# Seven products by whole batches: the last phase of an attention and feed-forward kernel, rearranged

## The chip, the cores and the metric

The kernel runs on one core of a Trainium2 chip. A core has TensorE (matrix products, results in PSUM), VectorE, ScalarE, GpSimd and DMA queues; each works through its own list of instructions, and semaphores tie the lists together. In profile lines they are PE (with PEld for its weight loads), DVE, ACT, POOL and SP. The metric is the device time of one execution in microseconds (us), as the median of several runs.

## What is computed

Routed attention is followed by a feed-forward block. Cut to what matters here:

```python
# attention: batch 4, heads 8, seq 768, head_dim 64; attn_out (4, 8, 768, 64)
x = attn_out.transpose(0, 2, 1, 3).reshape(3072, 512)
h = x @ w_in                                  # (3072, 512) @ (512, 2048)
g = h * (1.0 / (1.0 + np.exp(-1.702 * h)))    # a quick gelu
return (g @ w_out).astype(np.float32)         # (3072, 2048) @ (2048, 512)
```

Attention of all four batches and the feed-forward block of batch 0 lie in the earlier phases. The last phase, which is changed, does the feed-forward block of batches 1, 2 and 3. All matrix products are in float32; the profile has two matmul records for each one in the program.

## The kernel before

In the last phase both products are done in the way of Strassen and Winograd: each matrix is cut into 2 x 2 blocks, and seven products of blocks and of sums of blocks take the place of eight. A11 to A22 are the blocks of the left side, S1 to S4 sums of them; B11 to B22 and T1 to T4 the same of the right side; C11 to C22 are the blocks of the result. In the first layer A is w_in (by halves of the 2048 hidden features and of the 512 inputs) and B is x transposed (by halves of the inputs and of a batch's tokens). In the second layer A is the hidden layer g and B is w_out. P is 128, HALF 384, NF 16, FB 8, DM 512, DN 256, NH 3, B 4. A *group* is a batch and one of three parts of 128 token columns from both halves; there are nine groups.

```python
def sum_up(engine, A, S, side=0):
    if side == 0:
        todo = ((S[1], A[21], A[22], ALU.add),
                (S[2], S[1], A[11], ALU.subtract),
                (S[4], A[12], S[2], ALU.subtract),
                (S[3], A[11], A[21], ALU.subtract))
    else:
        todo = ...                       # cut: the four sums of a right side
    for o, a, b, op in todo:
        engine.tensor_tensor(out=o, in0=a, in1=b, op=op)

def seven(product, C):                   # the order of both layers
    def add(o, p, a):
        nc.vector.tensor_tensor(out=o, in0=p, in1=a, op=ALU.add)
    p = product(lambda A, S: A[11], lambda B, T: B[11])
    nc.scalar.copy(C[11], p)
    p = product(lambda A, S: S[2], lambda B, T: T[2])
    add(C[22], p, C[11])
    p = product(lambda A, S: S[1], lambda B, T: T[1])
    add(C[12], p, C[22])
    p = product(lambda A, S: S[3], lambda B, T: T[3])
    add(C[21], p, C[22]); add(C[22], p, C[12])
    yield 22
    p = product(lambda A, S: S[4], lambda B, T: B[22])
    add(C[12], p, C[12])
    yield 12
    ...                                  # cut: A22 T4 to C21, A12 B21 to C11

def first7(i, quad):                     # four chunks of 128 features, 128 columns
    ...
    def product(a, x):
        ps = ps_b.tile([P, 512], FP32, name="b")
        for f in range(4):
            for c in range(2):
                nc.tensor.matmul(out=ps[:, f * P:(f + 1) * P], lhsT=a(*ws[4 * quad + f, c]),
                                 rhs=x(*xs[c]), start=(c == 0), stop=(c == 1))
        return ps
    ...
    for k in seven(product, C):
        t = th.tile([P, 4 * P], FP32, name="th")
        gelu(C[k], t, C[k])   # ScalarE: tanh(1.702 h); VectorE: (tanh + 1) * h

def second7(i):
    ...
    def product(a, z):
        ps = bank()
        for f in range(FB):
            nc.tensor.matmul(out=ps[:, 0:DN], lhsT=a(*gs[f // 4])[:, f % 4 * P:(f % 4 + 1) * P],
                             rhs=z(*zs[f])[:, 0], start=(f == 0), stop=(f == FB - 1))
        return ps[:, 0:DN]
    for k in seven(product, C):
        ...                              # cut: store this quarter of the result

for c in range(2):
    sum_up(nc.vector, *W(c, 0, 4 * P))   # sums of w_in, kept for the whole phase
sums_x(0)
for c in range(2):
    sum_up(nc.vector, *W(c, 4 * P, FB * P))
sums_x(1)
while ffn:
    ffn.popleft()()                      # what is left of batch 0
...                                      # cut: ok and ok1, the check of the row sums
for f in range(0, FB, 2):
    sum_up(nc.gpsimd, *Z(f, f + 2), 1)   # sums of w_out
first7(0, 0)
for i in range(len(groups)):
    last = i == len(groups) - 1
    sums_g(i, 0)                         # VectorE: sums of g
    first7(i, 1)
    sums_g(i, 1)
    first7(i + 1, 0)
    sums_x(i + 2)
    if last:
        ...                              # cut: transpose of ok1, okt, bad
        is_bad = nc.values_load(bad[0:1, 0:1], min_val=0, max_val=1)
    second7(i)
```

The value is_bad decides at the end whether a general version runs in addition; with these inputs it does not. ScalarE's tanh and VectorE's product after it are the gelu of h / 2, since attention leaves x halved.

Of the kernel before, what the change touches and what calls it, by code (L numbers as in the profile page):

```python
# [8 lines left out]
FP32 = mybir.dt.float32  # L9
# [5 lines left out]
ALU = mybir.AluOpType  # L15
AX = mybir.AxisListType
# [22 lines left out]
def fast(  # L39
# [26 lines left out]
    nc = tc.nc  # L66

    B, H, S, D = q.shape
    NC = centroids.shape[1]
    DM, DF = moe_w_in.shape  # L70
# [36 lines left out]
    def bank():  # L107
        return ps_m.tile([P, 512], FP32, name="m")
# [117 lines left out]

    hot = hp1.tile([P, NJ * 4, 32], BF16, name="hot")
    nc.vector.memset(hot, 0.0)
    sums = const.tile([P, 2, 2 * NPAIR], FP32, name="sums")

# [240 lines left out]
    def check(g):  # L473


        rec = recs.pop(g)
        nc.scalar.activation(out=rec, in_=rec, func=AF.Copy,
                             accum_out=sums[:, 0, g:g + 1])
        nc.scalar.activation(out=rec, in_=rec, func=AF.Relu, bias=top[:, 0:1],
                             scale=-2.0 * LIMIT * LIMIT,  # L480
                             accum_out=sums[:, 1, g:g + 1])


    def gelu(g, t, h):

        nc.scalar.activation(out=t, in_=h, func=AF.Tanh, scale=1.702)  # L486
        nc.vector.scalar_tensor_tensor(out=g, in0=t, scalar=1.0, in1=h,  # L487
                                       op0=ALU.add, op1=ALU.mult)
# [111 lines left out]
    for t in range(NT + 2):  # L600
# [39 lines left out]
        if second_half and t % 2:  # L640
# [15 lines left out]
    FB = NF // 2  # L656
    DN = DM // 2
    sp = ctx.enter_context(tc.tile_pool(name="sp", bufs=1))
    tp = ctx.enter_context(tc.tile_pool(name="tp", bufs=2))
    gb = ctx.enter_context(tc.tile_pool(name="gb", bufs=18))  # L660
    th = ctx.enter_context(tc.tile_pool(name="th", bufs=1))
    ps_b = ctx.enter_context(tc.tile_pool(name="ps_b", bufs=5, space=PS))
    W_of = {(i, c): sp.tile([P, FB * P], FP32, name=f"W{i}{c}")
            for i in (1, 2, 4) for c in range(2)}
    Z_of = {i: sp.tile([P, FB, DN], FP32, name=f"Z{i}") for i in (2, 3, 4)}
    groups = [(b, n) for b in range(1, B) for n in range(NH)]

    def sum_up(engine, A, S, side=0):

        if side == 0:  # L670
            todo = ((S[1], A[21], A[22], ALU.add),
                    (S[2], S[1], A[11], ALU.subtract),
                    (S[4], A[12], S[2], ALU.subtract),
                    (S[3], A[11], A[21], ALU.subtract))
        else:
            todo = ((S[3], A[22], A[12], ALU.subtract),
                    (S[1], A[12], A[11], ALU.subtract),
                    (S[2], A[22], S[1], ALU.subtract),
                    (S[4], A[21], S[2], ALU.subtract))
        for o, a, b, op in todo:  # L680
            engine.tensor_tensor(out=o, in0=a, in1=b, op=op)  # L681

    def W(c, lo, hi):

        A = {10 * (r + 1) + m + 1: w_in[:, 2 * m + c, r * FB * P + lo:
                                        r * FB * P + hi]
             for r in range(2) for m in range(2)}
        S = {i: W_of[i, c][:, lo:hi] for i in (1, 2, 4)}
        S[3] = A[21]
        return A, S  # L690

    def Z(lo, hi):

        Bs = {10 * (r + 1) + m + 1: w_out[:, r * FB + lo:r * FB + hi,
                                          m * DN:(m + 1) * DN]
              for r in range(2) for m in range(2)}
        T = {i: Z_of[i][:, lo:hi] for i in (2, 3, 4)}
        T[1] = Bs[12]
        return Bs, T

    xs_of = {}

    def sums_x(i):

        if i >= len(groups):
            return
        b, n = groups[i]
        t = tp.tile([P, 2, 3, P], FP32, name="T")
        for c in range(2):
            Bs = {10 * (r + 1) + h + 1: xT_of[(2 * b + h) * HP + 2 * r + c][  # L710
                :, n * P:(n + 1) * P] for r in range(2) for h in range(2)}
            T = {k + 2: t[:, c, k] for k in range(3)}
            T[1] = Bs[12]
            sum_up(nc.vector, Bs, T, 1)
            xs_of[i, c] = Bs, T

    def seven(product, C):

        def add(o, p, a):
            nc.vector.tensor_tensor(out=o, in0=p, in1=a, op=ALU.add)  # L720

        p = product(lambda A, S: A[11], lambda B, T: B[11])
        nc.scalar.copy(C[11], p)  # L723
        p = product(lambda A, S: S[2], lambda B, T: T[2])
        add(C[22], p, C[11])
        p = product(lambda A, S: S[1], lambda B, T: T[1])
        add(C[12], p, C[22])
        p = product(lambda A, S: S[3], lambda B, T: T[3])
        add(C[21], p, C[22])
        add(C[22], p, C[12])  # L730
        yield 22
        p = product(lambda A, S: S[4], lambda B, T: B[22])
        add(C[12], p, C[12])
        yield 12
        p = product(lambda A, S: A[22], lambda B, T: T[4])
        add(C[21], p, C[21])
        yield 21
        p = product(lambda A, S: A[12], lambda B, T: B[21])
        add(C[11], p, C[11])
        yield 11  # L740

    g_of = {}

    def first7(i, quad):

        if i >= len(groups):
            return
        xs = [xs_of[i, c] for c in range(2)]
        ws = {(f, c): W(c, f * P, (f + 1) * P)
              for f in range(4 * quad, 4 * quad + 4) for c in range(2)}  # L750

        def product(a, x):
            ps = ps_b.tile([P, 512], FP32, name="b")
            for f in range(4):
                for c in range(2):
                    nc.tensor.matmul(out=ps[:, f * P:(f + 1) * P],  # L756
                                     lhsT=a(*ws[4 * quad + f, c]),
                                     rhs=x(*xs[c]),
                                     start=(c == 0), stop=(c == 1))
            return ps  # L760

        C = {k: gb.tile([P, 4 * P], FP32, name="g") for k in (22, 12, 21, 11)}
        for k in seven(product, C):
            t = th.tile([P, 4 * P], FP32, name="th")
            gelu(C[k], t, C[k])

        C[12], C[21] = C[21], C[12]
        g_of[i, quad] = C

    def sums_g(i, quad):  # L770
        if i >= len(groups):
            return
        A = g_of[i, quad]
        S = {k: gb.tile([P, 4 * P], FP32, name="g") for k in (1, 2, 4)}
        S[3] = A[21]
        sum_up(nc.vector, A, S)
        g_of[i, quad] = A, S

    def second7(i):
        b, n = groups[i]  # L780
        gs = [g_of.pop((i, quad)) for quad in range(2)]
        zs = [Z(f, f + 1) for f in range(FB)]
        ys = [gp.tile([P, 4 * P], FP32, name="g") for _ in range(2)]
        C = {10 * (h + 1) + m + 1: ys[h][:, m * DN:(m + 1) * DN]
             for h in range(2) for m in range(2)}

        def product(a, z):
            ps = bank()
            for f in range(FB):
                nc.tensor.matmul(  # L790
                    out=ps[:, 0:DN],
                    lhsT=a(*gs[f // 4])[:, f % 4 * P:(f % 4 + 1) * P],
                    rhs=z(*zs[f])[:, 0], start=(f == 0), stop=(f == FB - 1))
            return ps[:, 0:DN]

        for k in seven(product, C):
            h, m = k // 10 - 1, k % 10 - 1
            cols = slice(m * DN, (m + 1) * DN)
            nc.sync.dma_start(out=out_rows(b, h, n)[:, cols],
                              in_=ys[h][:, cols])  # L800

    for c in range(2):
        sum_up(nc.vector, *W(c, 0, 4 * P))
    sums_x(0)
    for c in range(2):
        sum_up(nc.vector, *W(c, 4 * P, FB * P))
    sums_x(1)
    while ffn:
        ffn.popleft()()

    ok = const.tile([P, 2, 2 * NPAIR], FP32, name="ok")
    nc.vector.tensor_scalar(out=ok, in0=sums, scalar1=LIMIT, scalar2=None,
                            op0=ALU.is_le)
    ok1 = const.tile([P, 1], FP32, name="ok1")
    nc.vector.tensor_reduce(out=ok1, in_=ok, axis=AX.XY, op=ALU.min)
    okt = const.tile([1, 1], FP32, name="okt")
    bad = const.tile([1, 1], I32, name="bad")
    for f in range(0, FB, 2):
        sum_up(nc.gpsimd, *Z(f, f + 2), 1)
    first7(0, 0)  # L820
    for i in range(len(groups)):
        last = i == len(groups) - 1
        sums_g(i, 0)
        first7(i, 1)
        sums_g(i, 1)
        first7(i + 1, 0)
        sums_x(i + 2)
        if last:
            ps = bank()
            nc.tensor.transpose(out=ps[0:1, 0:P], in_=ok1, identity=ident)  # L830
            nc.vector.tensor_reduce(out=okt, in_=ps[0:1, 0:P], axis=AX.X,
                                    op=ALU.min)
            nc.vector.tensor_scalar(out=bad, in0=okt, scalar1=-1.0,  # L833
                                    scalar2=1.0, op0=ALU.mult, op1=ALU.add)
            is_bad = nc.values_load(bad[0:1, 0:1], min_val=0, max_val=1)
        second7(i)
    return is_bad
@with_exitstack
def general(
# [436 lines left out]
```

## Time and profile before

| | |
|---|---|
| three runs | 1083.44, 1078.71, 1083.49 us; median 1083.44 us |
| profiled run | 1078.58 us; span from first to last instruction 1076.8 us |
| mean granted TensorE clock | 0.978 of full speed |
| TensorE busy over the span | 1009.8 us (94%) |
| VectorE | 690.0 us (64%) |
| ScalarE | 357.3 us (33%) |
| GpSimd | 319.8 us (30%) |
| 680.4 to 705.4 us, a first layer in the steady state | TensorE 25.01 us busy, VectorE 17.44, ScalarE 4.84, GpSimd 0 |
| 705.4 to 729.6 us, a second layer | TensorE 24.18 us busy, VectorE 7.35, ScalarE 1.63, GpSimd 0 |
| 593.4 to 608.3 us, the rest of batch 0 | TensorE 14.90 us busy, VectorE 14.61, GpSimd 11.42 |

A page shows how busy each engine was; the chain of waits leads back from the last instruction through what released each step, and so shows which engine the time belongs to. The timeline gives instructions in order with the idle time before each and its releaser. In lines of the timeline L756 is the first layer's matmul, L790 the second layer's, L720 an addition from PSUM, L486 and L487 the two halves of gelu, L681 a sum of blocks, L516 a first-layer product of batch 0 with 384 columns. Where an engine that has spare time sits idle, nothing is lost.

### The profile page before, as it was taken

The numbers are of one execution on the slowest core, as the hardware profiler recorded it, in microseconds if no ns is written. First come the engines' busy times: TensorE is split into PE (matmuls) and PEld (weight loads), VectorE is DVE, ScalarE is ACT, GpSimd is POOL, SyncE is SP. The second block draws the span as 40 slices with busy tenths as digits, with TensorE's granted clock in tenths as the row PEclk, the third lists the DMA queues.
The fourth block names the chain that finished last, engine by engine and source line by source line (L and its number), as shares of the span: only waits on it lengthen the run. The fifth ranks groups of instructions, "written<-read, shape, count | busy, mean of one in ns | idle before, by whom it ended". The sixth has DMA issues, their size and how long they took to land.

```text
span 1076.8 us, 14981 instructions
## 1 busy us (share of the span) xinstructions
PE 1009.8 (94%) x5918; PEld 684.8 (64%) x5918; DVE 690.0 (64%) x1077; ACT 357.3 (33%) x658; POOL 319.8 (30%) x184
## 2 busy tenths in 40 slices
PE   7878698999999999999998799999999999999977
PEld 4323353445544455444543399999899999999966
DVE  3899997336876787767877986546363635455341
ACT  4655554424555555555554011111020201111110
POOL 2654222213665556655667800000000000000000
PEclk9998899999999999999999899999999999999989
DMA  8423353112003310221000000000000000000000
GB/s 217 122 79 98 122 165 120 47 39 69 9 15 74 99 31 1 59 67 40 9 1 1 10 1 5 16 11 11 20 2 20 2 20 1 21 6 16 15 6 23
DMA packets 67423, 45.41 MB, mean 42 GB/s; under 512 B 52240, under 2 KB 62480, under 8 KB 67344
## 3 DMA queue, kind: packets, MB, share of 16 engines
q1 hardware_dynamic: 67200, 44.33, 14.5%
q8 instruction: 49, 0.80, 0.3%
q14 instruction: 30, 0.25, 0.1%
q10 hardware_dynamic: 144, 0.03, 0.0%
HBM read 38.04 MB, written 6.31 MB: 41 GB/s over the span
## 4 chain that ended last, share of the span: by engine, by line
PE 81%; DVE 14%; ACT 3%; issue 1%; DMA 1%; POOL 0%; SPq 0%; DVEq 0%; ACTq 0%; POOLq 0%
PE b L756 20%; PE m L790 20%; PE s L393 11%; PE o L450 9%; PE m L496 7%; PE m L545 4%; DVE short L465 3%; PE m L516 2%; PE m L271 2%; DVE A L429 2%; PE m L462 2%; DVE e L168 1%; PE m L285 1%; DVE W L681 1%; DVE e L180 1%
## 5 line engine op out<-in xcount | busy, mean ns | idle before, releaser
L439 POOL TENSOR_TENSOR sum<-sum,A 128x768 f32<-128x768 f32 x128 | 235.7, 1841 | 200.4 <-DVE A L429 104.5
L429 DVE SCALAR_TENSOR_TENSOR A<-qb,code,s 128x384 f32<-128x384 uint8 x288 | 157.7, 608 | 94.7 <-ACT s L418 79.6
L393 PE MATMUL s<-T,T 64*128 64x384 f32 x768 | 156.5, 519 | 13.2 <-ACT A L418 9.0
L450 PE MATMUL o<-A,inv 128*64 128x384 f32 x768 | 147.2, 502 | 1.1 <-DVE A L429 1.1
L790 PE MATMUL m<-w_out,g 128*128 128x256 f32 x576 | 132.7, 384 | 7.2 <-DVE bad L833 7.2
L418 ACT ACTIVATE s<-s 128x768 f32<-128x768 f32 x144 | 109.4, 793 | 83.4 <-PE s L393 72.7
L790 PEld LDWEIGHTS m<-w_out,g 128*128 128x128 f32 x576 | 110.5, 193 | 22.6 <-issue 7.4
L393 PEld LDWEIGHTS s<-T,T 64*128 64x128 f32 x768 | 65.3, 187 | 85.5 <-issue 22.8
L720 DVE TENSOR_TENSOR g<-m,g 128x256 f32<-128x256 f32 x63 | 26.8, 425 | 144.8 <-PE m L790 144.4
L486 ACT ACTIVATE th<-g 128x512 f32<-128x512 f32 x72 | 45.4, 630 | 198.2 <-DVE g L720 198.2
L450 PEld LDWEIGHTS o<-A,inv 128*64 128x64 f32 x768 | 47.1, 137 | 87.1 <-issue 80.9
L720 DVE TENSOR_TENSOR g<-b,g 128x512 f32<-128x512 f32 x126 | 85.7, 687 | 23.2 <-PE b L756 21.5
L790 PE MATMUL m<-Z,g 128*128 128x256 f32 x432 | 97.6, 379 | 0.0
L465 DVE RECIPROCAL short<-m 128x384 f32<-128x384 f32 x32 | 81.7, 2553 | 13.9 <-PE m L462 13.8
L790 PEld LDWEIGHTS m<-Z,g 128*128 128x128 f32 x432 | 82.1, 190 | 11.2
L439 POOL TENSOR_TENSOR sum<-A 128x768 f32<-128x768 f32 x32 | 59.6, 1862 | 92.7 <-ACT A L418 43.1
L487 DVE SCALAR_TENSOR_TENSOR g<-th,g 128x512 f32<-128x512 f32 x72 | 49.9, 693 | 54.7 <-ACT th L486 54.7
L756 PE MATMUL b<-x,W 128*128 128x128 f32 x576 | 70.9, 277 | 0.0
L756 PE MATMUL b<-T,w_in 128*128 128x128 f32 x576 | 70.2, 275 | 0.0
L756 PE MATMUL b<-x,w_in 128*128 128x128 f32 x576 | 68.8, 275 | 0.0
L723 ACT COPY g<-b 128x512 f32<-128x512 f32 x18 | 10.4, 577 | 175.0 <-PE b L756 175.0
L756 PEld LDWEIGHTS b<-x,W 128*128 128x128 f32 x576 | 68.0, 194 | 0.0
(103 smaller groups left out, 1199.1 us busy)
## 6 DMA issues: line engine op xcount, KB each, us to landing
raw<-in_moe_w_in_dram SPq DMA_DIRECT2D x16, 512.0 KB, 3.7
raw<-in_moe_w_out_dram SPq DMA_DIRECT2D x16, 512.0 KB, 3.6
in<-in_q_dram SPq DMA_DIRECT2D x32, 192.0 KB, 3.0
in<-in_k_dram SPq DMA_DIRECT2D x32, 192.0 KB, 3.8
inv<-in_v_dram SPq DMA_DIRECT2D x16, 384.0 KB, 4.1
out_dram<-g SPq DMA_DIRECT2D x36, 128.0 KB, 1.7
qb<-line SPq DMA_DIRECT2D x12, 192.0 KB, 3.2
out_dram<-y SPq DMA_DIRECT2D x6, 256.0 KB, 2.1
```

The lines of the kernel that those rows point to most:

```text
L393: nc.tensor.matmul(out=ps[:, a, 0:HALF], lhsT=T[p, 1][rows, kt * P:(kt + 1) * P], rhs=T[p, 0][rows, h * HALF:(h + 1) * HALF], start=True, ...
L418: nc.scalar.activation(out=A_of[u] if p < HP else s, in_=s, func=AF.Exp, scale=SCALE)
L429: nc.vector.scalar_tensor_tensor(out=A_of[u][:, a, :], in0=qcode[p][:, a, h * HALF:(h + 1) * HALF], scalar=code[p][:, kt % NH, 1, kt // NH ...
L439: nc.gpsimd.tensor_tensor(out=sum_of[g], in0=A_of[u - 1] if kt == 1 else sum_of[g], in1=A, op=ALU.add)
L450: nc.tensor.matmul(out=o_of[g][a * D:(a + 1) * D, 0:HALF], lhsT=v_in[p][:, a, kt, :], rhs=A[:, a, :], start=(kt == 0), stop=(kt == NJ - 1))
L465: nc.vector.reciprocal(out=rec, in_=ps[:, 0:HALF])
L486: nc.scalar.activation(out=t, in_=h, func=AF.Tanh, scale=1.702)
L487: nc.vector.scalar_tensor_tensor(out=g, in0=t, scalar=1.0, in1=h, op0=ALU.add, op1=ALU.mult)
L496: nc.tensor.matmul(out=ps[:, 0:DM], lhsT=g, rhs=w_out[:, f, :], start=(f == 0), stop=(f == NF - 1))
L720: nc.vector.tensor_tensor(out=o, in0=p, in1=a, op=ALU.add)
L756: nc.tensor.matmul(out=ps[:, f * P:(f + 1) * P], lhsT=a(*ws[4 * quad + f, c]), rhs=x(*xs[c]), start=(c == 0), stop=(c == 1))
L790: nc.tensor.matmul(out=ps[:, 0:DN], lhsT=a(*gs[f // 4])[:, f % 4 * P:(f % 4 + 1) * P], rhs=z(*zs[f])[:, 0], start=(f == 0), stop=(f == FB ...
```

## The change

The first layer is done for a whole half batch of tokens at once: 384 columns per matmul, one chunk f of features after the other, and the hidden layer of a whole batch lies in one buffer G. The three second layers of the batch follow. The sums of w_in are no longer kept for the phase: GpSimd makes them again for each batch, chunk by chunk, two chunks ahead, and in batch 1 it makes the sums of w_out between them. In the second layer the products without sums of g come first, so that VectorE can make the sums meanwhile. Gelu goes by blocks of 384. The check moves from the last group into the groups before. The attention part differs only in the name of one tile.

```diff
+    wq = ctx.enter_context(tc.tile_pool(name="wq", bufs=2))
-    W_of = {(i, c): sp.tile([P, FB * P], FP32, name=f"W{i}{c}")
-            for i in (1, 2, 4) for c in range(2)}
+    G = sp.tile([P, NF, 2, HALF], FP32, name="G")
 ...
+    def sums_w(i):
+        if i >= (B - 1) * FB:
+            return
+        f = i % FB
+        S = wq.tile([P, 3, 2, P], FP32, name="W")
 ...
+        if i < FB:
+            sums(nc.gpsimd, ((S[3], A11, "-", S[3]),))
+        sums(nc.gpsimd, ((S[2], A22, "-", S[3]), (S[1], S[2], "+", A11),
+                         (S[4], A12, "-", S[2])))
 ...
+    def first7(b, f, X, T):
+        S = w_of.pop((b - 1) * FB + f)
         def product(a, x):
             ps = ps_b.tile([P, 512], FP32, name="b")
+            for c in range(2):
+                nc.tensor.matmul(out=ps[:, 0:HALF], lhsT=a[:, c], rhs=x(c),
+                                 start=(c == 0), stop=(c == 1))
+            return ps[:, 0:HALF]
+        def finish(g):
+            gelu(g, th.tile([P, HALF], FP32, name="th"), g)
+        g1, g2 = G[:, f], G[:, f + FB]
+        p = product(A_in(0, 0, f), lambda c: X[0, 0, c])
+        nc.scalar.copy(g1[:, 0], p)
 ...  (products with S2, S1, S3, added to g2[:, 1], g1[:, 1], g2[:, 0], g2[:, 1])
+        p = product(S[4], lambda c: X[1, 1, c])
+        add(g1[:, 1], p, g1[:, 1])
+        finish(g2[:, 1])
+        p = product(A_in(1, 1, f), lambda c: T[4, c])
+        add(g2[:, 0], p, g2[:, 0])
+        finish(g1[:, 1])
+        p = product(A_in(0, 1, f), lambda c: X[1, 0, c])
+        add(g1[:, 0], p, g1[:, 0])
+        finish(g2[:, 0])
+        finish(g1[:, 0])
 ...
+    def second7(b, n, sg):
 ...
+        p = product(lambda q: A_out(0, 0, q, n), lambda f: Bz(0, 0, f))
+        nc.scalar.copy(C[11], p)
+        p12 = product(lambda q: A_out(0, 1, q, n), lambda f: Bz(1, 0, f))
+        p = product(lambda q: A_out(1, 1, q, n), lambda f: Tz(4, f))
+        nc.scalar.copy(C[21], p)
+        p = product(lambda q: sg[2, q], lambda f: Tz(2, f))
 ...  (then the products with S1, S3 and, last, S4)
-    for c in range(2):
-        sum_up(nc.vector, *W(c, 0, 4 * P))
-    sums_x(0)
-    for c in range(2):
-        sum_up(nc.vector, *W(c, 4 * P, FB * P))
-    sums_x(1)
+    sums_w(0)
+    XT = sums_x(1)
+    sums_w(1)
     while ffn:
         ffn.popleft()()
 ...
+    for b in range(1, B):
+        for f in range(FB):
+            if b == 1:
+                sums_z(f)
+            first7(b, f, *XT)
+            sums_w((b - 1) * FB + f + 2)
+        for n in range(NH):
+            sg = sums_g(n)
+            if (b, n) == (B - 1, 1):
+                ps = bank()
+                nc.tensor.transpose(out=ps[0:1, 0:P], in_=ok1, identity=ident)
 ...  (okt and bad from it, on VectorE)
+            if (b, n) == (B - 1, NH - 1):
+                is_bad = nc.values_load(bad[0:1, 0:1], min_val=0, max_val=1)
+            second7(b, n, sg)
+            if n == 1 and b < B - 1:
+                XT = sums_x(b + 1)
+            if (b, n) == (B - 1, 0):
 ...  (ok and ok1: the check of the row sums, on VectorE)
```

In sums_z GpSimd makes four sums of 256 elements of w_out for a chunk; in sums_x VectorE makes the eight sums of 384 elements of x for a batch; in sums_g it makes eight sums of 512 elements of G for a group. G11 in the prediction is what A_out(0, 0, q, n) names, the block g1[:, 0] of all chunks.

## The prediction

> **What bounds the kernel now.** I read the busy shares and slices first, to see whether one engine fills the last phase.
>
> ```profile
> PE   7878698999999999999998799999999999999977
> ...
> POOL 2654222213665556655667800000000000000000
> PEclk9998899999999999999999899999999999999989
> ```
>
> From slice 24 on (646 us) TensorE is full at full clock and GpSimd is empty; slices 21 to 22 (565 to 619 us, counted from 0) and the last two show holes. The chain of waits then gives the phase in pieces (start, length, what):
>
> ```profile
> 139.56 5.16 PE m L516 x16
> ...
> 618.15 38.06 PE b L756 x318
> 656.21 24.18 PE m L790 x112
> 680.38 25.01 PE b L756 x224
> 705.39 24.18 PE m L790 x112
> ```
>
> The phase is a TensorE stream: 25.01 us for the first layer's products of one group (224 records), 24.18 us for the second layer's (112 records). A group is 128 rows of both halves of a batch; there are nine. One record of 128 columns costs 25.01/224 = 111.7 ns, one of 256 columns 24.18/112 = 215.9 ns; the first line, from an earlier phase with 384 columns, gives 5.16/16 = 322.5 ns. Columns are thus not all that is paid: three of 128 cost 335 ns, one of 384 costs 322.5.
>
> The timeline around both holes (start, length, engine, line, operation, tiles, count, idle time before and its releaser) shows the rest:
>
> ```profile
> 609.99 1.35 DVE L681 TENSOR_TENSOR T<-x 128x128 f32<-128x128 f32 x1
> ...
> 614.07 0.80 PE L756 MATMUL b<-T,W 128*128 128x128 f32 x2 [3.93 <-DVE T L681]
> ...
> 618.15 3.36 PE L756 MATMUL b<-T,W 128*128 128x128 f32 x14 [3.28 <-DVE T L681]
> ...
> 621.30 2.64 PE L756 MATMUL b<-x,W 128*128 128x128 f32 x16
> ...
> 624.67 0.28 DVE L681 TENSOR_TENSOR T<-x 128x128 f32<-128x128 f32 x1
> ...
> 1044.49 6.12 PE L790 MATMUL m<-w_out,g 128*128 128x256 f32 x16 [7.18 <-DVE bad L833]
> 1050.23 3.43 PEld L790 LDWEIGHTS m<-Z,g 128*128 128x128 f32 x16
> 1050.44 3.62 PE L790 MATMUL m<-Z,g 128*128 128x256 f32 x16
> ```
>
> At the start TensorE waits twice for VectorE's sums, 3.93 + 3.28 = 7.2 us. At the end it waits 7.2 us for the last group's gelu, sums and the check. After each hole it is slow for a while: the 16 records at 1044.49 take 6.12 us instead of 3.62. The end costs 26.85 - 24.18 = 2.7 us that way. At the start the chain's 318 records take 38.06 us, where 318 x 111.7 ns is 35.5: 2.5 us. Also, the same 128-element VectorE sum takes 1.35 us while GpSimd sums and 0.28 us alone.
>
> **What the Trainium skill says.** "TensorE: Matmul & The Clock Gate", section "What's actually happening": idle time halves the array's clock and sustained work brings it back. The trace agrees: 6.12 against 3.62 us, with a granted clock of 0.91 over 1044 to 1071 us and 1.00 in the groups between. The same page, section "Back-to-back issue gap", adds about 2.5 ns to the column time of a warm matmul. That fits 322.5 and 215.9 ns, but not the 111.7 ns of a 128-column record; the trace decides. "SBUF — State Buffer", section "Terms": VectorE and GpSimd share a port pair that one holds for its whole instruction. The trace agrees for sums with both inputs in SBUF (1.35 against 0.28 us). VectorE's masks of attention, with one input in PSUM, take 0.55 us each (four in 2.19 at 577.9 us) wholly beside GpSimd sums, so for additions from PSUM I take no slowdown.
>
> **The change, part by part.**
>
> 1. *384 columns.* The first layer of a batch is now 8 chunks x 7 products x 2 parts of the contraction x 2 records = 224 records of 384 columns, where three groups had 672 of 128. Cost 224 x 322.5 ns = 72.2 us instead of 3 x 25.01 = 75.0; over three batches -8.4 us. The second layer keeps 9 x 24.18 = 217.6 us.
>
> 2. *Start.* The eight sums of w_in (13.5 us on VectorE, from 596.6 us) leave VectorE. GpSimd makes those of two chunks ahead: eight operations of 256 elements. Its 768-element sums take 1.84 us and an unopposed 512-element one took 1.27, so I estimate 0.72 us for 256. GpSimd is done with attention at 591.9; even if each operation alternates with a VectorE sum (0.72 + 0.56 = 1.28 us) it is through by 604. VectorE's first sums of x (eight of 384 elements) can start at 596.6 and end by 607. TensorE is still busy with batch 0's second layer until 608.3, and the first product needs no sums. Both waits should vanish, and the slow records with them: -7.2 - 2.5 = -9.7 us.
>
> 3. *Gelu and PSUM in the steady state.* Seven PSUM additions and four gelu operations per chunk. VectorE takes 425 ns for 256 and 687 for 512 elements, so some 556 for 384; gelu 693 at 512 scales to about 557. Per chunk 7 x 0.556 + 4 x 0.557 = 6.1 us, under TensorE's 28 x 0.3225 = 9.03. ScalarE needs under 3 us. With five PSUM banks, TensorE need not wait.
>
> 4. *Between the layers, three times.* The second layer begins with the product of unsummed G11, whose last chunk (f = 7) comes last from gelu. After TensorE's last first-layer product: addition 0.56, gelu 0.56, tanh about 0.5, gelu 0.56, with semaphores about 2.5 us. TensorE reaches that block after seven eighths of a 3.45 us product, at 3.0 us. So it should fit; with a GpSimd operation in the way it is late by up to 0.8 us. I charge 0.5 x 3 = +1.5 us. The sums of g (eight at 688 ns, 5.5 us) are first needed in the fourth product, 10.4 us in: hidden. The same holds between groups, even after the second group, where the next batch's sums of x (4.5 us) come first.
>
> 5. *End.* The last second layer no longer follows its own gelu; its sums lie behind three products. The 7.2 us of waiting and 2.7 us of slow records go: -9.9 us. The final addition and the store stay, with the 5.5 us from the last matmul to the end.
>
> 6. *The check.* Its two VectorE operations (0.19 + 0.22 us) now follow the last addition of group 0 of the last batch, and TensorE's transpose waits for them before the next group: addition 0.42, 0.41, semaphores and transpose, about +1.2 us. The register read stands one group later, when its value is long there; before, 0.57 us lay between the value and the next matmul, so +0.6 us.
>
> Sum: -8.4 - 9.7 - 9.9 + 1.5 + 1.2 + 0.6 = -24.7 us. As a cross-check, from TensorE's free moment: 608.3 + 216.7 + 217.6 + 3.3 + 5.5 = 1051.4 us of span, against 1076.8, or -25.4. Earlier phases keep their instruction order.
>
> **The rivals.**
>
> *VectorE becomes the bound in batch 1.* There GpSimd has eight operations per chunk (four for w_in, four for w_out), 8 x 0.72 = 5.8 of every 9.03 us, and gelu has both inputs in SBUF. If each gelu operation waits out a GpSimd one, VectorE needs 3.9 + 4 x 1.28 = 9.0 us per chunk, exactly TensorE's time; 10% more would cost 0.9 x 8 = 7 us. The doubled sums at 609 us speak for it; that GpSimd is free a third of the time, and five PSUM banks lie between, speaks against. Time: 1063 us. In batches 2 and 3 GpSimd has three operations per chunk, and this is no danger.
>
> *GpSimd comes late with the sums of w_in.* With two buffers a chunk's sums can start only when the chunk two before has passed its fifth product. Chunk 2's start at 6.5 us and are needed at 19.4: 13 us of slack for at most eight operations, 5.8 us alone and 10.2 in alternation. I reject it for a steady state; it would show up as waits for GpSimd and cost up to 1.2 us a chunk in batch 1, some 10 us in all.
>
> *The layer changes are worse than a spill of 0.5 us.* Three stalls of 3 us, each with slow matmuls after it, would cost 12 us: 1068 us. For it speaks one tanh buffer, so that tanh and gelu alternate; against it, the 2.5 us chain above, worked out with just that alternation.
>
> *Everything fits.* Without the three charges the gain is 28 us: 1053 us on the median's scale.
>
> **Range and chances.** The median before is 1083.44 us, but its runs lie between 1078.71 and 1083.49, and the profiled run was 1078.58. 1083.44 - 24.7 is 1058.7; from the profiled run it would be 1053.9. I put 1056. The low end, 1047, has everything fitting and a run of the faster kind; the high end, 1067, has one rival true. The 2% line is 1061.8, some 6 us above the centre, while the rivals cost 7 to 12: faster by over 2% 0.74, within 2% 0.23, slower 0.03.
>
> **What would show each step.** Part 1: 384-column pieces at 322 ns a record. Part 2: no wait of TensorE between 608 and 625 us. Part 3: VectorE near 70% in batch 1's first layer; at 95% or more the first rival holds. Part 4: waits for gelu under 1 us at three places. Part 5: the last second-layer stretch at 24.2 us without a hole before it. Part 6: two short TensorE waits in the last batch, both under 1.5 us. I would be wrong above all if a layer change leaves TensorE idle long enough to lower its clock, or if the sums on GpSimd slow gelu more than 0.72 us each.

## The result, and the profile after

The changed kernel takes 1054.45 us in the median of four runs (1050.77 to 1055.73), the one before 1083.47, with a fourth run (1078.71 to 1083.65): a ratio of 0.974, with a 95% interval of 0.970 to 0.977. The predicted 1056 us is 1.6 us off. The span of the profiled run fell from 1076.8 to 1048.9 us.

First the page of the changed kernel: busy shares, and TensorE, GpSimd and the granted clock in 40 slices.

```profile
PE 996.9 (95%) x4574; PEld 583.3 (56%) x4574; DVE 686.5 (65%) x1079; ACT 365.3 (35%) x697; POOL 389.3 (37%) x280
...
PE   7878798999999999999999899999999999999997
...
POOL 2655222223666456655567847600022100120000
PEclk9998899999999999999999999999999999999999
```

The holes at the start and at the end of the phase are gone, and so are the low digits of the clock there. TensorE's busy time fell by 13 us only; the rest of the gain was idle time. GpSimd is busier by 70 us, which by itself says nothing of the end. The chain of waits of the changed kernel says where the phase goes (start, length, what):

```profile
592.93 15.10 PE m L496 x32
608.03 72.24 PE b L733 x224
680.27 72.52 PE b L790 x336
...
969.79 24.19 PE b L790 x112
...
994.00 0.42 DVE y L724
994.42 0.11 DVE ok L850
...
994.56 0.23 DVE ok L853
...
994.83 0.27 PE m L836
995.10 48.36 PE b L790 x224
```

L733 is now the first layer's matmul, L790 the second layer's, L724 an addition from PSUM, L671 a sum of blocks. From the rest of batch 0 to the last matmul the chain leaves TensorE once, for the last addition of a group and the two operations of the check. Batches 2 and 3 repeat the lengths of batch 1. A batch's first layer takes 72.24 us for 224 records, 322.5 ns each; the second layers take 72.52 us for 336, 215.8 ns each.

For the experiments I use one number, the *phase time*, read from one profiled execution of each kernel: from TensorE's first record of the phase's first product to the end of its last matmul. Before it is 463.1 us (608.20 to 1071.34), after 435.6 (607.87 to 1043.46). It leaves out the first 600 us, whose length differs by some 4 us between runs of nearly the same code: the phase's first record starts at 607.7 to 612.2 us in the profiles of the changed kernel and its variants. The phase itself repeats closely: three kernels below with the same TensorE stream (after, a_no_gp, a_dve_w) agree to 0.01 us. The expectations count 435.4 for the changed kernel, from the chain's piece that starts 0.16 us after the record.

### The profile page after: what moved, and what is told of

Read it like the earlier page. It is cut to its first block, busy times and chain, and to the rows that moved or that the text cites. A ratio compares the mean times of both kernels' runs of the same rounds, so it can differ in the third digit from the quotient of the medians.

```text
span 1048.9 us, 12464 instructions
## 1 busy us (share of the span) xinstructions
PE 996.9 (95%) x4574; PEld 583.3 (56%) x4574; DVE 686.5 (65%) x1079; ACT 365.3 (35%) x697; POOL 389.3 (37%) x280
## 4 chain that ended last, share of the span: by engine, by line
PE 82%; DVE 12%; ACT 3%; issue 1%; DMA 1%; POOL 1%; SPq 0%; DVEq 0%; ACTq 0%; POOLq 0%
PE b L790 21%; PE b L733 21%; PE s L393 11%; PE o L450 9%; PE m L496 8%; PE m L545 4%; DVE short L465 3%; PE m L516 2%; DVE A L429 2%; PE m L271 2%; PE m L462 2%; DVE e L168 1%; PE m L285 1%; DVE e L180 1%; DVE w_in L186 1%
## 5 line engine op out<-in xcount | busy, mean ns | idle before, releaser
L724 DVE TENSOR_TENSOR G<-b,G 128x384 f32<-128x384 f32 x168 | 93.4, 556 | 51.8 <-PE b L733 45.0
L671 POOL TENSOR_TENSOR W<-w_in 128x256 f32<-128x256 f32 x24 | 17.7, 738 | 263.7 <-PE b L733 262.8
L724 DVE TENSOR_TENSOR y<-b,y 128x256 f32<-128x256 f32 x54 | 22.1, 423 | 130.0 <-PE b L790 93.8
L733 PE MATMUL b<-x,w_in 128*128 128x384 f32 x288 | 101.2, 486 | 0.0
L487 DVE SCALAR_TENSOR_TENSOR G<-th,G 128x384 f32<-128x384 f32 x96 | 68.6, 714 | 16.8 <-ACT th L486 14.2
L733 PEld LDWEIGHTS b<-x,w_in 128*128 128x128 f32 x288 | 54.7, 190 | 37.9 <-issue 0.5
L733 PE MATMUL b<-x,W 128*128 128x384 f32 x192 | 69.8, 486 | 0.0
L516 PE MATMUL m<-x,w_in 128*128 128x384 f32 x128 | 51.4, 560 | 15.5 <-ACT short L291 4.9
L790 PE MATMUL b<-Z,G 128*128 128x256 f32 x288 | 65.1, 379 | 0.0
L790 PE MATMUL b<-w_out,G 128*128 128x256 f32 x288 | 63.6, 379 | 0.0
L790 PEld LDWEIGHTS b<-w_out,G 128*128 128x128 f32 x288 | 54.6, 190 | 8.1
L496 PE MATMUL m<-w_out,g 128*128 128x512 f32 x120 | 58.7, 613 | 0.2 <-ACT T L276 0.2
```

The source lines that it names most:

```text
L496: nc.tensor.matmul(out=ps[:, 0:DM], lhsT=g, rhs=w_out[:, f, :], start=(f == 0), stop=(f == NF - 1))
L516: nc.tensor.matmul(out=ps[:, 0:HALF], lhsT=w_in[:, c, f * P:(f + 1) * P], rhs=xT[c], start=(c == 0), stop=(c == NCH - 1))
L733: nc.tensor.matmul(out=ps[:, 0:HALF], lhsT=a[:, c], rhs=x(c), start=(c == 0), stop=(c == 1))
L790: nc.tensor.matmul(out=ps[:, 0:DN], lhsT=a(f // 4)[:, f % 4], rhs=z(f), start=(f == 0), stop=(f == FB - 1))
```

## The experiments

The kernels named b_ are edits of the kernel before, those named a_ of the changed one. First the table, then each.

| run | edit | phase time, us | against its parent |
|---|---|---|---|
| before | | 463.1 | |
| b_start | sums of w_in on GpSimd | 463.1 | 0.0 |
| b_start_no_z | the same, sums of w_out left out | 452.9 | -10.2 |
| b_check | check one group earlier | 455.5 | -7.6 |
| b_both | b_start and b_check | 455.3 | -7.8 |
| after | | 435.6 | |
| a_128 | 128 columns again | 444.0 | +8.4 |
| a_check_last | check where it was | 443.3 | +7.7 |
| a_check_early | check's first part at the start | 434.6 | -1.0 |
| a_sums_first | products with sums first | 448.6 | +13.0 |
| a_no_gp | nearly no sums on GpSimd | 435.6 | 0.0 |
| a_dve_w | sums of w_in on VectorE, by chunks | 435.6 | 0.0 |
| a_z_up_front | sums of w_out all at the start | 436.9 | +1.3 |

**a_128: the columns alone.**

```diff
-            for c in range(2):
-                nc.tensor.matmul(out=ps[:, 0:HALF], lhsT=a[:, c], rhs=x(c), ...)
+            for n in range(NH):
+                for c in range(2):
+                    at = slice(n * P, (n + 1) * P)
+                    nc.tensor.matmul(out=ps[:, at], lhsT=a[:, c], rhs=x(c)[:, at], ...)
```

> The changed kernel, with each matmul of the first layer cut into three of 128 columns, weights loaded again for each. Theory: the columns alone are worth 672 x (111.7 - 322.5/3) = 2.8 us a batch, so 435.4 + 8.4 = 443.8 us from the first product to the last matmul. Rival: the gain of the columns was really that TensorE ran without interruption, and 128-column records in this order cost no more than a third of a 384-column one: under 438 us.

Measured 444.0 us, +8.4. The chain of waits of this run has the same shape as the changed kernel's, with longer first layers:

```profile
611.86 75.04 PE b L735 x672
```

75.04/672 is 111.7 ns a record, the time of before, though nothing interrupts the stream and the order is the new one. So the price belongs to the 128-column record (each with its weight load). In device time the run took 1061.93 us, a ratio to before of 0.982 (0.981 to 0.984); the changed kernel has 0.974.

**b_start: the sums of w_in taken off VectorE, in the kernel before.**

```diff
-        sum_up(nc.vector, *W(c, 0, 4 * P))
+        sum_up(nc.gpsimd, *W(c, 0, 4 * P))
     sums_x(0)
-        sum_up(nc.vector, *W(c, 4 * P, FB * P))
-    sums_x(1)
+        sum_up(nc.gpsimd, *W(c, 4 * P, FB * P))
 ...
     first7(0, 0)
+    sums_x(1)
```

> The kernel before with one thing changed: the sums of w_in are made by GpSimd instead of VectorE, and the second group's sums of x come after the first group's first products. Measured from the first product of the last phase to the last matmul, the kernel before takes 463.1 us. Theory: the start's loss is VectorE's sums of w_in, 7.2 us of waiting and 2.5 us of slow records, so 453.4 us. Rival: the sums are merely late on another engine (sixteen of 512 elements on GpSimd, 1.27 to 1.6 us each, share the port with the sums of x): TensorE waits for GpSimd instead, and the time stays above 459 us.

The edit does two things: it also puts the second group's sums of x behind the first products. Measured 463.1 us: the rival's time, though the wait is for VectorE and not for GpSimd. The two waits for sums are gone and one about as long as both has taken their place. The timeline of this run (L487 is gelu, L681 a sum of blocks) shows why:

```profile
619.44 1.27 POOL L681 TENSOR_TENSOR w_out<-w_out 128x512 f32<-128x512 f32 x1
619.59 1.67 DVE L487 SCALAR_TENSOR_TENSOR g<-th,g 128x512 f32<-128x512 f32 x1 [0.76 <-ACT th L486]
...
627.25 1.35 DVE L681 TENSOR_TENSOR T<-x 128x128 f32<-128x128 f32 x1
...
635.61 2.74 DVE L681 TENSOR_TENSOR g<-g 128x512 f32<-128x512 f32 x4
638.27 2.80 DVE L720 TENSOR_TENSOR g<-b,g 128x512 f32<-128x512 f32 x4
639.01 3.36 PE L756 MATMUL b<-x,w_in 128*128 128x128 f32 x14 [7.97 <-DVE g L720]
```

GpSimd's sums run until 635 us, and beside them gelu takes 1.67 us instead of 0.69 and a sum of x 1.3 instead of 0.28. VectorE falls behind; the additions at 638 us, which free PSUM banks, come late, and TensorE waits 7.97 us for them. So taking the sums off VectorE, done in this way, does not cure the start. Two causes were left: GpSimd's load, or the order of VectorE's work, in which sums of x and of g stand between the additions of two quads.

**b_start_no_z: the same, and GpSimd's sums of w_out left out.**

```diff
-    for f in range(0, FB, 2):
-        sum_up(nc.gpsimd, *Z(f, f + 2), 1)
+    for i in (2, 3, 4):
+        nc.gpsimd.memset(Z_of[i], 0.0)
```

> The kernel before with GpSimd making the sums of w_in, as in the earlier edit of the start, and GpSimd's sums of w_out left out (zeroed), so the result is not the reference's. In the earlier edit TensorE's wait came back, 8.0 us, behind VectorE. Theory: it came back because GpSimd's 512-element sums ran on and doubled VectorE's gelu (1.67 us instead of 0.69) and sums of x (1.3 instead of 0.28); without them no wait is left at the start and no slow records: 453.4 us from the first product to the last matmul, against 462.9. Rival: it came back because the second group's sums of x and the first sums of g stand between the additions of two quads on VectorE; then a wait of 4 us or more stays, 458 us or more.

Measured 452.9 us, no wait of TensorE at the start, gelu back to 0.69 us and the sums of x to 0.28; the order of VectorE's work is that of b_start. The chain of waits runs from the rest of batch 0 into the products without leaving TensorE:

```profile
595.01 15.10 PE m L496 x32
610.11 37.52 PE b L756 x336
```

From the first gelu to the additions that free the banks VectorE takes 11.8 us here (619.40 to 631.18) and 21.2 in b_start (617.11 to 638.27). The new order alone therefore makes no wait; with GpSimd's load it makes one of 7.97 us. Whether the same load would have hurt with the sums of x up front, as before, was not tried. (The sums of w_out are needed; the run only tells where the wait came from.)

**a_dve_w: does it matter which engine makes the sums of w_in?** All chunk-by-chunk sums of w_in go to VectorE, at the same places; the sums of w_out stay on GpSimd.

```diff
-            sums(nc.gpsimd, ((S[3], A11, "-", S[3]),))
-        sums(nc.gpsimd, ((S[2], A22, "-", S[3]), (S[1], S[2], "+", A11),
+            sums(nc.vector, ((S[3], A11, "-", S[3]),))
+        sums(nc.vector, ((S[2], A22, "-", S[3]), (S[1], S[2], "+", A11),
```

> The changed kernel with all its chunk-by-chunk sums of w_in made by VectorE instead of GpSimd, in the same places of the program. Theory: what cured the start is that only one or two chunks' sums stand ahead of the first products, not the engine; VectorE then has 6.2 + 4 x 0.42 = 7.9 us, with some port waits 8.3, of the 9.03 us of a chunk, and TensorE sees nothing: 435.4 to 436.5 us from the first product to the last matmul. Rival: VectorE is too full for it and becomes the bound, or the start's wait returns: 438 us or more.

Measured 435.6 us, no new wait. The busy time in the first layer of batch 1 (stretch, length, then busy us and count for PE, PEld, DVE, ACT, POOL, then clock, DMA share and GB/s):

```profile
611.02:683.26 72.24, 72.24 (x225) 42.56 (x225) 58.80 (x114) 19.53 (x40) 17.52 (x22) 1.00 0.01 4
```

VectorE is 81% busy there and 72 to 74% in the first layers of batches 2 and 3, and TensorE's only wait is the one for the check. In this kernel the engine that makes the sums of w_in does not matter. That the start is cured by having only two chunks' sums ahead of the first products fits this, but no run puts all eight chunks' sums there.

**a_no_gp: does sharing the port cost anything?** From the third chunk on the first two chunks' sums of w_in are used again, and the sums of w_out are left out and zeroed.

```diff
+        S = wq.tile([P, 3, 2, P], FP32, name="W") if i < 2 else None
+        if i >= 2:
+            w_of[i] = dict(keep[i % 2])
+            w_of[i][3] = A_in(1, 0, f)
+            return
 ...
-            if b == 1:
-                sums_z(f)
+            if (b, f) == (1, 0):
+                for i in (2, 3, 4):
+                    nc.gpsimd.memset(Z_of[i], 0.0)
```

> The changed kernel without GpSimd's sums from the third chunk on: the sums of w_in of the first two chunks are used again for all later ones, and the sums of w_out are left out and zeroed, so the result is not the reference's. Theory: GpSimd's sums slow gelu on VectorE (714 ns against 557) but stay off TensorE's path: 435.4 us from the first product to the last matmul, and gelu back to 557 ns. Rival: sharing the port costs TensorE time after all: 433 us or less.

Measured 435.6 us, the changed kernel's time. The groups of instructions of both show gelu, with count, busy us and mean ns; first the changed kernel, then this run:

```profile
L487 DVE SCALAR_TENSOR_TENSOR G<-th,G 128x384 f32<-128x384 f32 x96 | 68.6, 714 | 16.8 <-ACT th L486 14.2
```

```profile
L487 DVE SCALAR_TENSOR_TENSOR G<-th,G 128x384 f32<-128x384 f32 x96 | 53.1, 553 | 14.2 <-ACT th L486 14.2
```

Gelu is on average 161 ns slower with GpSimd's sums, 15.5 us over the phase, and none of it reaches TensorE.

**a_z_up_front: the sums of w_out ahead of the products.**

```diff
-            if b == 1:
-                sums_z(f)
+            if (b, f) == (1, 0):
+                for i in range(FB):
+                    sums_z(i)
```

> The changed kernel with GpSimd's 32 sums of w_out all ahead of the first products, as before had its sixteen larger ones, instead of four per chunk between the sums of w_in. Theory: the sums of w_in of chunk 2 then stand behind 32 operations of 0.73 to 1.07 us and are ready some 631 us into a span in which TensorE wants them at 627: one wait for GpSimd of 0 to 4 us, with no slow records if it is short: 435.4 to 440 us from the first product to the last matmul. Rival: GpSimd's order is of no account, since it has time in plenty: no wait for GpSimd at all, 435.4 us.

Measured 436.9 us. In the timeline of this run the sums of w_in for chunk 2 stand behind those of w_out:

```profile
629.91 1.07 POOL L671 TENSOR_TENSOR Z<-w_out,Z 128x256 f32<-128x256 f32 x1
...
632.72 1.56 PE L733 MATMUL b<-T,W 128*128 128x384 f32 x4 [1.03 <-POOL W L671]
```

One wait of 1.0 us, as expected; the rival had none. The place between the chunks matters, but for little here.

**b_check: the check one group earlier, in the kernel before.**

```diff
-        if last:
+        if i == len(groups) - 2:
             ps = bank()
             ...                          # transpose of ok1, okt, bad
+        if last:
             is_bad = nc.values_load(bad[0:1, 0:1], min_val=0, max_val=1)
```

> The kernel before with one thing changed: the transpose of the check and the two VectorE operations after it stand before the second to last second layer, and the register read alone before the last. Theory: the hole at the end is the check, which stood behind the last gelu and sums on VectorE. TensorE then runs half of the first product, waits some 1.9 us for gelu, and its clock stays up: 5.3 + 2.7 us less, 455.1 us from the first product to the last matmul instead of 463.1. Rival: gelu and sums of the last group hold TensorE whatever the check does, and only the order of products of the changed kernel cures it: a hole of 3.6 us or more remains, the slow records too, and the time is 459.5 us or more.

Measured 455.5 us, -7.6. TensorE's timeline at the end of this run:

```profile
1039.05 1.89 PE L790 MATMUL m<-w_out,g 128*128 128x256 f32 x8
1042.95 1.99 PE L790 MATMUL m<-w_out,g 128*128 128x256 f32 x8 [2.01 <-DVE g L487]
1044.78 3.40 PE L790 MATMUL m<-Z,g 128*128 128x256 f32 x15
```

The wait is 2.0 us for gelu instead of 7.2 for the check, and no slow stretch follows: the eight records after it take 1.83 us from start to start, where 8 x 215.9 ns is 1.73. Most of the end's loss was the place of a few small instructions.

**a_check_last: the check back at its old place, in the changed kernel.**

```diff
-            if (b, n) == (B - 1, 1):
+            if (b, n) == (B - 1, NH - 1):
                 ps = bank()              # transpose of ok1, okt, bad
```

> The changed kernel, with the transpose of the check and its two small VectorE operations moved to where the kernel before had them, ahead of the last second layer. They then stand behind the last group's sums of g on VectorE, and TensorE's register read waits for them. Theory: wait of addition 0.42 + sums 5.5 + check 0.41 + 0.57 = 6.9 us, some 2.6 us of slow records after it, less the 1.1 us that the check costs now: 435.4 + 8.4 = 443.8 us from the first product to the last matmul. Rival: the order of products took the hole away, and the place of the check counts for little: under 437 us.

Measured 443.3 us, +7.7. Timeline of TensorE:

```profile
1026.60 9.03 PE L790 MATMUL b<-w_out,G 128*128 128x256 f32 x32 [6.62 <-DVE bad L839]
```

and the same records in the changed kernel:

```profile
1019.12 7.07 PE L790 MATMUL b<-w_out,G 128*128 128x256 f32 x32
```

The old hole is back, in the new order of products, and the 32 records after it take 9.03 us instead of 7.07.

**a_check_early: the check's first part at the start of the phase.**

```diff
+    ok = const.tile([P, 2, 2 * NPAIR], FP32, name="ok")
+    ...                                  # ok and ok1, right after the rest of batch 0
     okt = const.tile([1, 1], FP32, name="okt")
 ...
-            if (b, n) == (B - 1, 0):
-                ...                      # ok and ok1
```

> The changed kernel, with the first two operations of the check (0.19 and 0.22 us of VectorE) back at the start of the phase, where VectorE has time. Theory: the one wait left in the phase goes, 435.4 - 0.9 = 434.5 us from the first product to the last matmul (TensorE keeps the 0.27 us transpose). Rival: the transpose then waits for the last addition or the next bank just as long: 435.4 us.

Measured 434.6 us, -1.0, with no wait of TensorE in the phase. In device time it is 1053.71 us, a ratio to before of 0.975 (0.973 to 0.977): 1 us can't be told in device time, as the changed kernel's runs spread over 5 us.

**b_both: both edits of the kernel before.**

> The two edits of the kernel before together. Theory: they add up, 463.1 - 9.7 - 8.0 = 445.4 us from the first product to the last matmul, with 384 columns worth the rest to the changed kernel's 435.4 less some 1.5 us. In device time about 1.6% less than before. Rival, in which each hole is refilled by the next wait: 455 us or more.

Measured 455.3 us, the rival's time: b_check's gain and nothing more, as b_start gives nothing. The ratio to before is 0.993 (0.992 to 0.995).

**a_sums_first: the old order of the second layer's products.**

```diff
         p = product(lambda q: A_out(0, 0, q, n), lambda f: Bz(0, 0, f))
         nc.scalar.copy(C[11], p)
-        p12 = product(lambda q: A_out(0, 1, q, n), lambda f: Bz(1, 0, f))
-        p = product(lambda q: A_out(1, 1, q, n), lambda f: Tz(4, f))
-        nc.scalar.copy(C[21], p)
         p = product(lambda q: sg[2, q], lambda f: Tz(2, f))
 ...  (S1, S3, S4, then the two without sums)
```

> The changed kernel with the products of the second layer in the order of before: G11, then the four with sums of g, then the two without. Theory: at each of three layer changes the sums are late by 0.55 us and then 0.9 us; after the sums of x of the next batch, twice, by 3.0 and 0.9 us: 4.4 + 7.8 = 12.2 us, and up to 5 us more if the 3 us holes slow the clock. So 447.6 to 452.6 us from the first product to the last matmul. Rival: VectorE keeps ahead in any order, as it did between groups before: under 437 us.

Measured 448.6 us, +13.0. TensorE's timeline, first at a layer change, then after the sums of x of the next batch:

```profile
684.14 1.99 PE L790 MATMUL b<-Z,g 128*128 128x256 f32 x8 [0.56 <-DVE g L671]
686.80 1.99 PE L790 MATMUL b<-Z,g 128*128 128x256 f32 x8 [0.66 <-DVE g L671]
...
736.57 1.99 PE L790 MATMUL b<-Z,g 128*128 128x256 f32 x8 [2.88 <-DVE g L671]
```

After each of these waits the listing gives eight records 1.99 us, as in b_check, so the clock stayed up in this execution. TensorE waits nine times for sums, 10.2 us in all; the other 2.8 us come to some 0.3 us for each wait. The order of products gains nothing over the kernel before; it pays for what whole batches would otherwise cost.

## Why the prediction was right, step by step

The sum was right, a little on the cautious side: 24.7 us predicted, 27.9 in the span and 29.0 between the medians. That 1056 us lies only 1.6 from the result owes something to luck: the sum taken from the median before gives 1058.7, and 1056 was set between that and a figure from one run that had been 5 us shorter. On the same scale the rival "everything fits" is 1083.44 - 28.0 = 1055.4 us, not the 1053 given there, and it is the one that came nearest.

*Part 1, columns.* Right to a tenth: 72.24 us a batch against 72.2, and a_128 gives the 8.4 us back. The issue gap cited beside it fits less directly than the prediction says. In the Trainium skill, "TensorE: Matmul & The Clock Gate", section "Back-to-back issue gap", the gap of a single warm matmul is N/2.4 + 2.5 ns for N columns, which is 162.5 ns for 384; the measured 322.5 and 215.9 ns fit only with twice that column time. The two records themselves give it: 106.6 ns more for 128 columns more.

*Part 2, start.* Both waits and the slow records went. The loss was 10.3 us and not 9.7: the 336 first-layer records ahead of the phase's first second layer take 48.0 us in the kernel before (608.20 to 656.21) and 37.7 in b_start_no_z. The prediction left out the two records between the waits, which its own fence shows at 0.80 us where 2 x 111.7 ns is 0.22. The reason put first, that the eight sums "leave VectorE", fell: in b_start they leave it and nothing is won, in a_dve_w they return to it and nothing is lost. What b_start and b_start_no_z show is that GpSimd's large sums beside VectorE cost the time. In the kernel before they did so too; its timeline has a sum of w_in beside them and one later, alone:

```profile
598.38 1.64 DVE L681 TENSOR_TENSOR W<-W,w_in 128x512 f32<-128x512 f32 x1
...
620.08 0.69 DVE L681 TENSOR_TENSOR W<-W,w_in 128x512 f32<-128x512 f32 x1
```

An estimate from these traces: undisturbed, the first eight sums of w_in and of x would take some 7.8 us from 596.6 and be done by 605, before TensorE wants them. No run took the sums of w_out alone out of the kernel before. The prediction read the slowed VectorE sums at 609 us rightly, but used them only for the changed kernel.

*Part 3, steady state.* Right: VectorE 51.5 of 72.2 us in batch 1's first layer, 71% where about 70 was named, additions of 384 elements at 556 ns, and 558 in a_no_gp without GpSimd's sums, so these additions from PSUM are not slowed, as assumed. (The masks from which this was taken lay beside GpSimd's sums for 1.85 of their 2.19 us, not wholly.) The first rival has its mechanism (gelu at 749 ns in batch 1, 714 over the phase) but not its effect: a_no_gp shows that it costs nothing, and a_dve_w that VectorE can be 81% busy. The second, GpSimd late with the sums of w_in, did not come: TensorE never waits for GpSimd in the changed kernel.

*Part 4, layer changes.* The charge of 1.5 us was too high: nothing is lost. The timeline of the changed kernel, around the end of the first layer at 680.27 us:

```profile
679.47 0.73 POOL L671 TENSOR_TENSOR W<-w_in,W 128x256 f32<-128x256 f32 x1
679.51 1.10 DVE L487 SCALAR_TENSOR_TENSOR G<-th,G 128x384 f32<-128x384 f32 x1
...
680.53 0.55 DVE L724 TENSOR_TENSOR G<-b,G 128x384 f32<-128x384 f32 x1
...
682.35 0.56 DVE L487 SCALAR_TENSOR_TENSOR G<-th,G 128x384 f32<-128x384 f32 x1 [0.59 <-ACT th L486]
```

The last gelu is done at 682.91, 2.64 us after the last first-layer product; TensorE needs it at 3.0, by the prediction's reckoning. It fits by some 0.4 us. GpSimd does get in the way, but of the gelu before, which takes 1.10 us instead of 0.56 and so holds the addition back from 680.27 to 680.53. The third rival, stalls of 3 us at the layer changes, did not come; even with the old order of products the waits are 0.56 and 0.66 us at the first of them (a_sums_first).

*Part 5, end.* Right in size; the reason named was the smaller part. The prediction put the loss to the last group's gelu and sums, with the check beside them, and the cure to the order of products. b_check and a_check_last show that the place of the check alone decides 7.6 to 7.7 of the 9.9 us, in either order. Without it the old order waits 2.0 us, for gelu (b_check).

*Part 6, check.* The 1.2 us charged for its first part is 1.1 in the chain (994.00 to 995.10 with the transpose), and a_check_early takes away 1.0 of it. The 0.6 us for the register read did not come: the last second layer follows the one before without a gap. Before, the 0.57 us followed a value that had just been made.

The phase time fell by 27.5 us, 2.8 more than the sum of the steps. The charges overrated 1.5 + 0.6 + 0.1 us of it, and the start was underrated by 0.6. The other 0.4 us of the span lies outside the phase.

## What to carry to other kernels

When an operation is moved to a second engine that shares a port with the first, count what it does to the work that stays: in b_start large sums on GpSimd more than doubled VectorE's two-input operations and gave the whole gain back, while the sums of w_in in small pieces between chunks were free on either engine. Look for small instructions that the in-order list of a busy engine puts behind long work, and for what waits on them: three tiny ones, the check's transpose and what follows it, cost 7.7 us in the wrong place. After a restructuring, put first what needs no preparation; it is worth measuring by putting the old order back.

## What the runs showed of the hardware

The length of a wait did not alone decide whether the granted clock fell after it. Two profiles have the same wait at the same place of the attention part, first the changed kernel, then b_check:

```profile
63.11 2.93 PE L393 MATMUL s<-T,T 64*128 64x384 f32 x8 [3.01 <-ACT A L418]
```

```profile
63.03 1.62 PE L393 MATMUL s<-T,T 64*128 64x384 f32 x8 [3.01 <-ACT A L418]
```

Over these eight records the granted clock was 0.50 in the first and 1.00 in the second; from 58 to 60 us it was 1.00 in both. In the last phase waits of 2.01 us (b_check) and 2.88 us (a_sums_first, twice) left it at 1.00, while one of 2.68 us was followed by 0.50 (b_check):

```profile
614.76 0.80 PE L756 MATMUL b<-T,W 128*128 128x128 f32 x2 [2.68 <-DVE T L681]
```

Every wait of 3.28 us or more in that phase was followed by a lower clock: after 6.62 us (a_check_last) 32 records of 256 columns took 9.03 us instead of 7.07. What decides between waits of equal length stays open, so a short wait that cost no clock here may cost it in another execution.

A 128-column record costs 111.7 ns in two quite different orders, 4.2 ns more than a third of a 384-column record (107.5).

VectorE operations with both inputs in SBUF took longer beside GpSimd's sums, by up to some three quarters of one GpSimd operation: gelu of 512 elements went from 0.69 to 1.67 us beside 512-element sums of 1.27 us (b_start), gelu of 384 elements from 0.56 to at most 1.10 beside 256-element sums of 0.73 (changed kernel, batch 1). That smaller sums on GpSimd cost VectorE less fits these two cases; no run changes the size alone.
